# A two-pass expert layer on one core: one plain unit fewer at the start of pass one, and half of x's sums moved to VectorE

## The chip, the cores and the metric

One core of a Trainium2 chip runs the whole kernel. The metric is the time on the device in microseconds (us) of one execution; lower is better. TensorE (PE) multiplies, with its weight loads shown apart as PEld; VectorE (DVE), ScalarE (ACT) and GpSimd (POOL) do the rest; SyncE (SP) issues the transfers. Each engine works through its own instructions in the order in which they stand.

## The reference

Causal attention with decay makes x, of 2304 tokens by 512. A gate then makes P by eight rounds of normalising over experts and over tokens, and eight experts are summed:

```python
    logits = x @ w_gate
    P = np.exp(logits - logits.max())
    for _ in range(8):
        P /= P.sum(1, keepdims=True) + 1e-09
        P /= P.sum(0, keepdims=True) + 1e-09
        P *= N / E
    for e in range(E):                       # E = 8; w1 512 x 1024, w2 1024 x 512
        h = np.maximum(x @ w1[e], 0.0)
        out += P[:, e:e + 1] * (h @ w2[e])
```

## The kernel before

Every float32 product is made of three products of rounded parts (hi by hi, hi by lo, lo by hi). ScalarE makes the hi part of an operand with a copy, and VectorE or GpSimd makes the lo part by subtracting it.

The tokens are done in three passes of 768. Work goes by units: a unit is one expert e and one quarter fb of its hidden width (256 columns), so a pass has 32 units. For pass one two units (e0, fb0 and fb1) are done during the attention. Then comes the loop that this change touches: `work` holds the 30 units that are left of pass one, m = 0 for (e0, fb2), m = 1 for (e0, fb3), m = 2 for (e1, fb0) and so on.

A unit has a first product (x by w1, then relu) and a second one (h by w2, added into `acc`). In program order unit m makes its first product, then `second(*late)` makes the second product of unit m - 1. The first product comes in two kinds:

- `first_plain` (L1268) does 48 matmuls of 128x384, straight from the split w1 in `early_w["w1"]`.
- `first_fast` (L1278) does Winograd's form of Strassen's scheme: seven products of six matmuls, 42 in all. It needs sums of blocks of w1 (`weight_sums`, four instructions on GpSimd, and `split_sums`, which puts their parts into the tiles of `early_w["w1"]` and the plain blocks into `wa`), and sums of blocks of x (`token_sums`, eight instructions for each half c of the columns, and `part_sums`, which splits the four sums into the tiles `t`, here named t_4214 for c = 0 and t_4237 for c = 1). Both halves of x's sums go through one tile, `ts`.

`PLAIN` (L1374) says how many units use the plain kind. For a fast unit, `keep_w1` stores the split blocks of w1 in DRAM, and pass two and three load them from there; for the units that were not kept, `prepare_w1` makes them during pass two.

PSUM banks: a first product uses four banks in turn (`FIRST`), each free again when relu and `hl` (the lo part of h, on VectorE) have read it. The second product has six tiles of six matmuls, which use three banks in turn while e is below 2 (`GATING`): the fourth tile can begin when VectorE has added the first to `acc`, the fifth when it has added the second.

The gate is computed in between by a generator, `gate_weights`, of 51 steps. `go_on()` does one step; `first_plain` calls it four times, `second` six times, `first_fast` never. Ahead of the second product of (2, 0), at m = 7, what is left of the generator is done at once, as that product needs `prob`. Its last steps are the eighth round (`pc` on TensorE, four small instructions on VectorE that end in `prob`) and three groups of transposes of `prob` into the bank `pt` (L1182), each copied by ScalarE.

From pass two on, an own planner (`arrange`) writes the order of the instructions. Up to there the framework orders them by its own estimates, except those that are pinned.

Of the kernel before, what the change touches and what calls it, by code (L numbers as in the profile page):

```python
# [144 lines left out]
def act_sbuf(n): return 0.1 + n / 1200  # L145
# [80 lines left out]
def attention_then_moe(  # L226
# [11 lines left out]
    nc = tc.nc  # L238
# [132 lines left out]
    def step(rank, on, run, **kw):  # L371
        s = Step(rank, on, run, **kw)
        steps.append(s)
        return s
# [647 lines left out]
    with tc.manual_schedule():  # L1022
# [22 lines left out]
        a = step(-1.0, {"ACT": act_sbuf(S)}, cum_hi, after=[cum_done])  # L1045
# [42 lines left out]
    KH = KC // 2  # L1088
# [96 lines left out]
            nc.sync.dma_start(out=p_d[:, a:a + DM], in_=ps[0:E])  # L1185
            yield

    def token_sums(g, c):

        def part(k, t):  # L1190
            s = (slice(None), 2 * k + c, slice(g + t * HT, g + (t + 1) * HT))
            return x_hi[s].bitcast(F32), x_lo[s].bitcast(F32)
        (h11, l11), (h12, l12), (h21, l21), (h22, l22) = part(0, 0), part(0, 1), part(1, 0), part(1, 1)
        t = up.tile([P, 4, HT], F32, tag="ts", name="ts")
        v2, v1, v3, v4 = (t[:, n] for n in range(4))
        def pinned(**kw):
            tc.keep_in_program_order(nc.gpsimd.tensor_tensor(**kw))

        pinned(out=v3, in0=h12, in1=l12, op=ALU.add)
        pinned(out=v2, in0=h22, in1=l22, op=ALU.add)  # L1200
        yield t
        pinned(out=v1, in0=v3, in1=h11, op=ALU.subtract)
        pinned(out=v1, in0=v1, in1=l11, op=ALU.subtract)
        yield t
        pinned(out=v3, in0=v2, in1=v3, op=ALU.subtract)
        pinned(out=v2, in0=v2, in1=v1, op=ALU.subtract)
        yield t
        pinned(out=v4, in0=h21, in1=v2, op=ALU.subtract)
        pinned(out=v4, in0=v4, in1=l21, op=ALU.add)
        yield t  # L1210

    def part_sums(n, c, t):
        if t_of[n][c] is None:
            t_of[1][0] = turns_p.tile([P, 2, 4, HT], F32R, tag="turns", name="t2")
        hi, lo = (t_of[n][c][:, x] for x in range(2))
        for m in range(0, 4, 2):
            tc.keep_in_program_order(nc.scalar.copy(out=hi[:, m:m + 2], in_=t[:, m:m + 2]))
            for x in range(m, m + 2):
                tc.keep_in_program_order(
                    nc.gpsimd.tensor_tensor(out=lo[:, x], in0=t[:, x], in1=hi[:, x].bitcast(F32), op=ALU.subtract)  # L1220
                )

    def raw(nm, e, fb):
        tags = {"w1": "rw", "w2": "rq"}[nm]
        return [load_half(e, fb, nm, n, wr_p.tile([P, HALF], F32, tag=f"{tags}{n}", name="w")) for n in range(2)]

    def split_whole(nm, rs, lo_on, ws=early_w):

        hi, lo = ws[nm]
        for n, r in enumerate(rs):  # L1230
            s = slice(n * r.shape[1], (n + 1) * r.shape[1])
            nc.scalar.copy(out=hi[:, s], in_=r)  # L1232
            a = lo_on.tensor_tensor(out=lo[:, s], in0=r, in1=hi[:, s].bitcast(F32), op=ALU.subtract)  # L1233
            if lo_on is nc.gpsimd:
                tc.keep_in_program_order(a)

    def weight_sums(rs):
        t = up.tile([P, 4, KH, P], F32, tag="ws", name="ws")
        (a11, a21), (a12, a22) = ([r[:, :, n * P:(n + 1) * P] for n in range(2)] for r in rs)
        tt = nc.gpsimd.tensor_tensor  # L1240
        tc.keep_in_program_order(tt(out=t[:, 2], in0=a11, in1=a21, op=ALU.subtract))
        tc.keep_in_program_order(tt(out=t[:, 0], in0=a21, in1=a22, op=ALU.add))
        tt(out=t[:, 1], in0=t[:, 0], in1=a11, op=ALU.subtract)
        tt(out=t[:, 3], in0=a12, in1=t[:, 1], op=ALU.subtract)
        return t

    def split_sums(rs, t):
        hi, lo = wa
        k1 = rs[1].rearrange("p c (i f) -> p i c f", f=P)
        nc.scalar.copy(out=hi[:, 0], in_=rs[0][:, :, 0:P])  # L1250
        nc.scalar.copy(out=wsum[0], in_=t)  # L1251
        nc.scalar.copy(out=hi[:, 1:3], in_=k1)
        nc.gpsimd.tensor_tensor(out=lo[:, 0], in0=rs[0][:, :, 0:P], in1=hi[:, 0].bitcast(F32), op=ALU.subtract)
        for n in range(4):
            nc.gpsimd.tensor_tensor(  # L1255
                out=wsum[1][:, n], in0=t[:, n], in1=wsum[0][:, n].bitcast(F32), op=ALU.subtract
            )
        for n in range(2):
            nc.gpsimd.tensor_tensor(out=lo[:, 1 + n], in0=k1[:, n], in1=hi[:, 1 + n].bitcast(F32), op=ALU.subtract)
# [4 lines left out]
    def go_on():  # L1264
        if pending and next(pending[0], True):
            pending.pop(0)

    def first_plain(segs, hts):  # L1268
        for n, (g, w) in enumerate(segs):
            for ft in range(FB):  # L1270
                ph = bank(FIRST, [P, 512], "ph")
                hidden(ph, early_w, ft, g, w, range(KC))
                hh, hl = hts[ft][n]
                relu_hi(hh, ph, w)
                relu_lo(hl, hh, ph, w)
                go_on()
# [66 lines left out]
    def weigh(e, i):  # L1343
        to = (acc, acc_1)[e][i]
        nc.scalar.activation(out=to, in_=to, func=AF.Copy, scale=prob[:, i, e:e + 1])
# [5 lines left out]
    def second(n, e, fb, segs, hts, ws):  # L1351
        tags = GATING if e < 2 else SECOND
        tiles = [(m, g // P + tt, tt) for m, (g, w) in enumerate(segs) for tt in range(w // P)]
        for k, (m, t, tt) in enumerate(tiles):
            po = bank(tags, [P, DM], "po")
            combine(po, ws, [hts[ft][m] for ft in range(FB)], tt, range(FB))
            add_to(po, e, fb, t)
            if later_lo and k in (1, 3):
                relu_lo(*later_lo.pop(0))
            go_on()  # L1360
# [4 lines left out]
    def keep_w1(e, fb):  # L1365
        d = w1_d[e, fb] = dram.tile([len(COMBOS), P, 2, KH * P], F32, name=f"w1d{e}{fb}")
        for x in range(2):
            for ts, a, z in ((wa, 0, 3), (wsum, 3, 7)):
                nc.sync.dma_start(
                    out=d[a:z, :, x].rearrange("s p f -> p s f"),  # L1370
                    in_=ts[x].rearrange("p s k f -> p s (k f)").bitcast(F32),
                )

    PLAIN = 3  # L1374
    halves = [(0, HT), (HT, HT)]
    work = [(0, e, fb, halves) for e in range(E) for fb in range(NB)][EARLY:]
    gated = [w[:3] for w in work].index((0, 2, 0))
# [6 lines left out]
    for m, (n, e, fb, segs) in enumerate(work):  # L1384
        fast, fast_next = m >= PLAIN, m + 1 >= PLAIN
        last = m + 1 == len(work)
        if not last:
            r1 = raw("w1", *work[m + 1][1:3])
        r2 = raw("w2", e, fb)
        if m < KH:  # L1390
            sums = token_sums(0, m)
            for t in sums:
                pass
        if m == 0:
            pending.append(gate_weights())
            go_on()
        hts = hts_of[m % 2]
        if not last and fast_next:
            ws = weight_sums(r1)
        if fast:  # L1400
            first_fast(n, segs[0][0], hts, parts[m] + (t,) if m in parts and parts[m][1] else ())
        else:
            first_plain(segs, hts)
        if m < KH:
            part_sums(0, m, t)
        if not last:
            if fast_next:
                split_sums(r1, ws)
                keep_w1(*work[m + 1][1:3])
            else:  # L1410
                split_whole("w1", r1, nc.vector)
        if m in starts:
            sums = token_sums(2 * starts[m][0] * HT, starts[m][1])
            t = next(sums)
        elif any(m - k in starts for k in (1, 2, 3)):
            next(sums)
        if m in parts and not parts[m][1]:
            part_sums(*parts[m], t)
        ws = early_w
        if last:  # L1420
            ws = {"w2": [t.rearrange("p s f -> p (s f)").rearrange("p (t d) -> p t d", d=DM) for t in early_w["w1"]]}
            split_whole("w2", r2, nc.gpsimd, ws)
        if late:
            if late[:3] == (0, 2, 0):
                while pending:
                    go_on()
                for i in range(PT):
                    weigh(0, i)
            second(*late)
        if 0 <= m - 2 - gated < PT:  # L1430
            join(m - 2 - gated)
        if not last:
            split_whole("w2", r2, nc.gpsimd if fast else nc.vector)
        late = (n, e, fb, segs, hts, ws)
# [652 lines left out]
```

## Time and profile before

| | us |
|---|---|
| median of 3 runs (lowest, highest) | 1630.55 (1630.13, 1631.98) |
| time of the profiled execution | 1630.41 |
| its span in the trace | 1628.6 |
| TensorE busy in the span | 1619.9 |
| VectorE, ScalarE, GpSimd busy | 1310.4, 767.3, 1122.2 |

The profiled execution is 1.8 us longer than its span, and 0.14 us shorter than the median. An engine that is busy for less than the span matters where TensorE has to wait for it.

### The profile page before, as it was taken

What the parts mean: (1) busy time and instruction counts of PE and PEld (TensorE: products, weight loads), DVE (VectorE), ACT (ScalarE), POOL (GpSimd) and SP (SyncE); (2) the same over time, 40 slices, a digit from 0 to 9 for tenths busy, and PEclk for the clock granted to TensorE, in tenths of its full rate; (3) what the DMA queues carried; (4) which work ended last, traced back from release to release, by engine and by line L of the source; (5) the groups of instructions that cost most, each with busy time, mean ns of one, the idle gap of its engine ahead of it and who ended that gap; (6) DMA issues with size and microseconds to landing.
All of it is one profiled execution on the core that took longest, in us unless ns stands there. A gap on an engine that the chain in (4) does not pass through costs nothing.

```text
span 1628.6 us, 29751 instructions
## 1 busy us (share of the span) xinstructions
PE 1619.9 (99%) x9641; PEld 1534.1 (94%) x9641; DVE 1310.4 (80%) x2742; ACT 767.3 (47%) x1918; POOL 1122.2 (69%) x1431
## 2 busy tenths in 40 slices
PE   8999999999999999999999999999999999999999
PEld 7888889989899899899999999999999999999998
DVE  8888778776676776788898888878988888788887
ACT  8887743443333333344454444444444444344443
POOL 6556385777788887778777767666666666566675
PEclk9999999999999999999999999999999999999999
DMA  6666325655566656576777776657665555565552
GB/s 154 157 159 160 92 64 175 185 178 185 181 197 184 193 185 209 181 233 192 229 222 220 221 224 201 187 175 218 197 198 162 171 178 170 164 173 171 168 167 70
DMA packets 257025, 291.24 MB, mean 179 GB/s; under 512 B 76291, under 2 KB 168686, under 8 KB 256870
## 3 DMA queue, kind: packets, MB, share of 16 engines
q1 hardware_dynamic: 256438, 288.94, 59.5%
q8 instruction: 77, 1.26, 0.3%
q14 instruction: 78, 0.64, 0.1%
q10 hardware_dynamic: 432, 0.39, 0.1%
HBM read 222.43 MB, written 66.83 MB: 178 GB/s over the span
## 4 chain that ended last, share of the span: by engine, by line
PE 98%; ACT 0%; POOL 0%; DVE 0%; DMA 0%; issue 0%; SPq 0%
PE bankA L1838 28%; PE bankA L1736 20%; PE po L924 16%; PE ph L1292 12%; PE bankM L1736 9%; PE pv L823 3%; PE ph L904 2%; PE pt L775 2%; PE ps L614 2%; PE pq L496 1%; PE ps L660 1%; PE bankA L1889 1%; PE pt L779 0%; PE ps L607 0%; PE bankA L1922 0%; PE pg L858 0%
## 5 line engine op out<-in xcount | busy, mean ns | idle before, releaser
L1847 DVE TENSOR_TENSOR sum<-bankA,sum 128x384 f32<-128x384 f32 x406 | 224.3, 553 | 52.9 <-PE bankA L1838 51.4
L1736 PE MATMUL bankA<-t,wn 128*128 128x384 f32 x1314 | 248.3, 334 | 0.0
L924 PE MATMUL po<-early_w,hh 128*128 128x512 f32 x768 | 239.1, 392 | 0.0
L1736 PEld LDWEIGHTS bankA<-t,wn 128*128 128x128 f32 x1314 | 229.4, 188 | 0.0
L924 PEld LDWEIGHTS po<-early_w,hh 128*128 128x128 f32 x768 | 142.4, 188 | 28.7 <-issue 0.7
L1666 POOL TENSOR_TENSOR fourw<-w 128x256 f32<-128x256 f32 x124 | 91.7, 740 | 92.2 <-DMA w<-in_moe_w_dram 92.2
L924 PE MATMUL po<-early_w,hl 128*128 128x512 f32 x384 | 150.3, 391 | 0.0
L1298 DVE TENSOR_TENSOR u<-ph,u 128x384 f32<-128x384 f32 x189 | 101.9, 552 | 56.8 <-PE ph L1292 53.2
L1337 DVE SCALAR_TENSOR_TENSOR acc<-po,prob,acc 128x512 f32<-128x512 f32 x144 | 106.6, 747 | 50.5 <-PE po L924 48.8
L1838 PE MATMUL bankA<-xhi,early_w 128*128 128x384 f32 x576 | 128.3, 334 | 0.0
L1255 POOL TENSOR_TENSOR early_w<-ws,early_w 128x256 fp32r<-128x256 f32 x108 | 93.9, 898 | 39.7 <-ACT early_w L1251 38.5
L1736 PE MATMUL bankM<-xhi,wn 128*128 128x384 f32 x424 | 119.0, 334 | 0.0
L1232 ACT CAST early_w<-w 128x512 fp32r<-128x512 f32 x66 | 41.0, 622 | 161.1 <-issue 137.9
L1838 PE MATMUL bankA<-xlo,early_w 128*128 128x384 f32 x522 | 116.8, 335 | 0.0
L1529 POOL TENSOR_TENSOR w2n<-fourw,w2n 128x256 fp32r<-128x256 f32 x105 | 79.6, 761 | 43.2 <-PE bankA L1838 21.5
L1838 PE MATMUL bankA<-xhi,w2n 128*128 128x384 f32 x480 | 108.9, 334 | 0.0
L1233 POOL TENSOR_TENSOR early_w<-w,early_w 128x512 fp32r<-128x512 f32 x56 | 71.9, 1305 | 44.8 <-ACT early_w L1232 44.8
L1838 PEld LDWEIGHTS bankA<-xhi,early_w 128*128 128x128 f32 x576 | 102.4, 188 | 0.0
L1838 PE MATMUL bankA<-xlo,w2n 128*128 128x384 f32 x438 | 99.4, 334 | 0.0
L910 ACT ACTIVATE hh<-u 128x384 fp32r<-128x384 f32 x108 | 56.1, 522 | 91.4 <-DVE u L1298 91.3
L1529 POOL TENSOR_TENSOR early_w<-w,early_w 128x256 fp32r<-128x256 f32 x96 | 72.4, 760 | 37.7 <-ACT early_w L1524 37.7
L1529 POOL TENSOR_TENSOR early_w<-fourw,early_w 128x256 fp32r<-128x256 f32 x117 | 89.5, 772 | 12.0 <-ACT early_w L1524 11.3
(332 smaller groups left out, 4518.6 us busy)
## 6 DMA issues: line engine op xcount, KB each, us to landing
wn<-w1d SPq DMA_DIRECT2D x440, 256.0 KB
w<-in_moe_w_dram SPq DMA_DIRECT2D x266, 256.0 KB
w1d<-early_w SPq DMA_DIRECT2D x54, 512.0 KB
w1d<-wa SPq DMA_DIRECT2D x54, 384.0 KB
w1d<-four SPq DMA_DIRECT2D x70, 128.0 KB
dn<-cum_d SPq DMA_DIRECT2D x14, 576.0 KB
pb<-p_d SPq DMA_DIRECT2D x16, 384.0 KB
q<-in_q_dram SPq DMA_DIRECT2D x32, 128.0 KB
```

The lines of the kernel that those rows point to most:

```text
L910: nc.scalar.activation(out=hh[:, 0:w], in_=ph[:, 0:w], func=AF.Relu)
L924: nc.tensor.matmul(po[:, cols], ht[:, ts], wt[:, ft, cols], start=(ft == 0 and n == 0), stop=(ft == FB - 1 and n == 2))
L1233: a = lo_on.tensor_tensor(out=lo[:, s], in0=r, in1=hi[:, s].bitcast(F32), op=ALU.subtract)
L1255: nc.gpsimd.tensor_tensor(out=wsum[1][:, n], in0=t[:, n], in1=wsum[0][:, n].bitcast(F32), op=ALU.subtract)
L1292: nc.tensor.matmul(ps, ws[y][:, c], xs[z], start=(c == 0 and m == 0), stop=(c == KH - 1 and m == 2))
L1298: nc.vector.tensor_tensor(out=out, in0=in0, in1=in1, op=ALU.add)
L1337: a = nc.vector.scalar_tensor_tensor(out=to, in0=po, scalar=prob[:, t, e:e + 1], in1=to, op0=ALU.mult, op1=ALU.add)
L1529: eng(e).tensor_tensor(out=dst(1), in0=src(), in1=dst(0).bitcast(F32), op=ALU.subtract)
L1666: eng(en).tensor_tensor(out=vs[o](), in0=a(), in1=b(), op=op)
L1736: nc.tensor.matmul(ps, wt[:, y, c * P:(c + 1) * P], x[z], start=(start and c == 0 and m == 0), stop=(c == KH - 1 and m == 2), skip_group_c ...
L1838: nc.tensor.matmul(at_(b)[:, 0:HT], at_(w)[y][:, k * P:(k + 1) * P], at_(h)[:, z], start=(i == 0), stop=(i == 5))
L1847: nc.vector.tensor_tensor(out=to, in0=at_(b)[:, 0:HT], in1=to, op=ALU.add)
```

## The change

Two plain units in place of three, so m = 2 becomes a fast unit. Its first product needs x's sums one unit earlier. The first half's sums (c = 0) are made by VectorE at m = 0; the second half's are made by GpSimd at m = 0 too, straight behind the split of the first half, and no longer at m = 1. The w1 of unit 2 is stored by `keep_w1`, so pass two has one `prepare_w1` less.

```diff
-    def token_sums(g, c):
+    def token_sums(g, c, on=nc.gpsimd):
...
         def pinned(**kw):
-            tc.keep_in_program_order(nc.gpsimd.tensor_tensor(**kw))
+            a = on.tensor_tensor(**kw)
+            if on is nc.gpsimd:
+                tc.keep_in_program_order(a)
...
-    PLAIN = 3
+    PLAIN = 2
...
-        if m < KH:
-            sums = token_sums(0, m)
+        if m == 0:
+            sums = token_sums(0, m, nc.vector)
             for t in sums:
                 pass
...
-        if m < KH:
-            part_sums(0, m, t)
+        if m == 0:
+            part_sums(0, 0, t)
+            for t in token_sums(0, 1):
+                pass
+            part_sums(0, 1, t)
```

Line numbers of the changed kernel are 2 higher from L1197 on, so L1222 there is L1220 before.

**GpSimd, units 0 and 1.** Before, from the first half's sums to the second half's parts (ts: sums of x; t: their lo parts):

```order
L1197 TENSOR_TENSOR ts<-xhi,xlo 128x384 x2
L1197 TENSOR_TENSOR ts<-ts,xhi 128x384
L1197 TENSOR_TENSOR ts<-ts,xlo 128x384
L1197 TENSOR_TENSOR ts<-ts 128x384 x2
L1197 TENSOR_TENSOR ts<-xhi,ts 128x384
L1197 TENSOR_TENSOR ts<-ts,xlo 128x384
L1220 TENSOR_TENSOR t_4214<-ts,t_4214 128x384 x4
```

Those six rows of sums and one of parts follow once more for t_4237. Now the first half's sums are gone from here, and three lo parts of unit 2's blocks of w1 (wa) stand among the second half's sums:

```order
L1222 TENSOR_TENSOR t_4214<-ts,t_4214 128x384 x4
L1197 TENSOR_TENSOR ts<-xhi,xlo 128x384 x2
L1197 TENSOR_TENSOR ts<-ts,xhi 128x384
L1255 TENSOR_TENSOR wa_4236<-w,wa_4235 128x256
L1197 TENSOR_TENSOR ts<-ts,xlo 128x384
L1197 TENSOR_TENSOR ts<-ts 128x384
L1261 TENSOR_TENSOR wa_4236<-w,wa_4235 128x256
L1197 TENSOR_TENSOR ts<-ts 128x384
L1261 TENSOR_TENSOR wa_4236<-w,wa_4235 128x256
L1197 TENSOR_TENSOR ts<-xhi,ts 128x384
L1197 TENSOR_TENSOR ts<-ts,xlo 128x384
L1222 TENSOR_TENSOR t_4237<-ts,t_4237 128x384 x4
```

Behind these come the four sums of unit 2's w1 (ws) and then the four lo parts of them (early_w_110<-ws), as before they did for unit 3.

**ScalarE, the same units.** Before, from unit 0's last relu on (hh: relu of a first product; the CAST of t: the hi parts of x's sums, two at a time; hh100, hh110, hh101 and hh111 belong to unit 1):

```order
L910 ACTIVATE hh011_4244<-ph_4331 128x384
L1217 CAST t0_4214<-ts_4270 128x768 x2
L910 ACTIVATE hh100_4246<-ph_4398 128x384
L1156 ACTIVATE prob_78<-lg_4279,ma_4415 128x144
L910 ACTIVATE hh110_4250<-ph_4426 128x384
L910 ACTIVATE hh101_4248<-ph_4441 128x384
L1232 CAST early_w10_109<-w_4381 128x512
L1232 CAST early_w10_109<-w_4383 128x512
L910 ACTIVATE hh111_4252<-ph_4456 128x384
L1217 CAST t1_4237<-ts_4389 128x768 x2
```

And now:

```order
L910 ACTIVATE hh011_4244<-ph_4331 128x384
L1219 CAST t0_4214<-ts_4270 128x768 x2
L910 ACTIVATE hh100_4246<-ph_4409 128x384
L1252 CAST wa0_4235<-w_4396 128x256
L1156 ACTIVATE prob_78<-lg_4279,ma_4426 128x144
L1254 CAST wa0_4235<-w_4398 128x512
L910 ACTIVATE hh110_4250<-ph_4437 128x384
L1219 CAST t1_4237<-ts_4373 128x768 x2
L910 ACTIVATE hh101_4248<-ph_4452 128x384
L910 ACTIVATE hh111_4252<-ph_4467 128x384
L1253 CAST early_w10_109<-ws_4404 128x1024
```

The two CASTs of t1 now stand ahead of the last two relus of unit 1. On VectorE hl101 and hl111, which read those relus, stand right ahead of the first two adds of unit 0's second product into acc, as they did before.

**TensorE, the gate's eighth round.** Now, in the second product of (2, 0) (pc: the gate's eighth round; pt: the first transposes of prob; po: tiles of the second product):

```order
L1171 MATMUL pc_5488<-cs_5353,ones_77 128x8
L924 MATMUL po_5524<-early_w20_111,hh_4238 128x512
L924 MATMUL po_5524<-early_w21_112,hh_4238 128x512
L924 MATMUL po_5524<-early_w20_111,hl_4239 128x512
L924 MATMUL po_5524<-early_w20_111,hh_4242 128x512
L924 MATMUL po_5524<-early_w21_112,hh_4242 128x512
L924 MATMUL po_5524<-early_w20_111,hl_4243 128x512
L924 MATMUL po_5532<-early_w20_111,hh_4238 128x512
L924 MATMUL po_5532<-early_w21_112,hh_4238 128x512
L924 MATMUL po_5532<-early_w20_111,hl_4239 128x512
L924 MATMUL po_5532<-early_w20_111,hh_4242 128x512
L1182 MATMUL pt_5494<-ident_75,prob_78 8x128 x4
```

Before, the same two stood in the second product one unit ahead of that one (from pc to the first transposes):

```order
L1171 MATMUL pc_5339<-cs_5196,ones_77 128x8
L924 MATMUL po_5345<-early_w20_111,hh101_4248 128x512
L924 MATMUL po_5345<-early_w21_112,hh101_4248 128x512
L924 MATMUL po_5345<-early_w20_111,hl101_4249 128x512
L924 MATMUL po_5345<-early_w20_111,hh111_4252 128x512
L924 MATMUL po_5345<-early_w21_112,hh111_4252 128x512
L924 MATMUL po_5345<-early_w20_111,hl111_4253 128x512
L924 MATMUL po_5362<-early_w20_111,hh101_4248 128x512
L924 MATMUL po_5362<-early_w21_112,hh101_4248 128x512
L1182 MATMUL pt_5354<-ident_75,prob_78 8x128 x4
```

The eighth round has moved by one unit, to the product that itself needs prob. On VectorE the four small instructions that end in prob now stand between and behind the last two hl of the first product just ahead.

## Rows read from the trace of the kernel before

**Rows 1.** The chain that ended last, by engine, shares of the span.

```profile
PE 98%; ACT 0%; POOL 0%; DVE 0%; DMA 0%; issue 0%; SPq 0%
```

**Rows 2.** Busy time by stretch, TensorE alone: stretch, length, busy (instructions), clock, DMA.

```profile
700.00:1600.00 900.00, 899.96 (x5200) 1.00 0.64 190
```

**Rows 3.** Timeline of TensorE, units 0 to 3: start, length, instruction.

```profile
230.85 0.63 PE L924 MATMUL po<-early_w,hh 128*128 128x512 f32 x2
...
235.22 0.62 PE L924 MATMUL po<-early_w,hh 128*128 128x512 f32 x2
...
239.32 0.33 PE L904 MATMUL ph<-xhi,early_w 128*128 128x384 f32 x1
...
257.42 3.28 PE L1292 MATMUL ph<-t,early_w 128*128 128x384 f32 x18
```

**Rows 4.** Timeline of ScalarE, the same units; in brackets idle time before, and releaser.

```profile
221.59 0.48 ACT L910 ACTIVATE hh<-ph 128x384 fp32r<-128x384 f32 x1
221.97 0.82 ACT L1217 CAST t<-ts 128x768 fp32r<-128x768 f32 x1
...
234.34 0.84 ACT L1217 CAST t<-ts 128x768 fp32r<-128x768 f32 x1 [2.42 <-POOL ts L1197]
...
247.96 1.05 ACT L1251 CAST early_w<-ws 128x1024 fp32r<-128x1024 f32 x1 [1.46 <-PE ph L904]
```

**Rows 5.** Timeline of GpSimd, the same units.

```profile
213.85 2.43 POOL L1197 TENSOR_TENSOR ts<-xhi,xlo 128x384 f32<-128x384 f32 x2
...
222.89 4.37 POOL L1220 TENSOR_TENSOR t<-ts,t 128x384 fp32r<-128x384 f32 x4
227.34 2.05 POOL L1197 TENSOR_TENSOR ts<-xhi,xlo 128x384 f32<-128x384 f32 x2
...
231.41 2.90 POOL L1197 TENSOR_TENSOR ts<-ts 128x384 f32<-128x384 f32 x2
...
236.45 4.09 POOL L1220 TENSOR_TENSOR t<-ts,t 128x384 fp32r<-128x384 f32 x4
...
249.09 2.82 POOL L1255 TENSOR_TENSOR early_w<-ws,early_w 128x256 fp32r<-128x256 f32 x4 [2.46 <-ACT early_w L1251]
251.99 0.74 POOL L1241 TENSOR_TENSOR ws<-w 128x256 f32<-128x256 f32 x1
```

**Rows 6.** VectorE: its timeline, then two lines' own durations (min/median/max ns).

```profile
230.53 2.91 DVE L1233 TENSOR_TENSOR early_w<-w,early_w 128x512 fp32r<-128x512 f32 x2 [0.48 <-ACT early_w L1232]
...
249.43 0.56 DVE L913 SCALAR_TENSOR_TENSOR hl<-ph,hh 128x384 fp32r<-128x384 f32 x1 [1.97 <-ACT hh L910]
249.90 0.68 DVE L1334 TENSOR_TENSOR acc<-po,acc 128x512 f32<-128x512 f32 x1
...
L1233 DVE TENSOR_TENSOR early_w<-w,early_w x10: 676/1063/1503, 211.7 to 257.7; 128x512 fp32r<-128x512 f32 x10
...
L1571 DVE TENSOR_TENSOR four<-four,xlo x1: 906/906/906, 695.1 to 695.1; 128x384 f32<-128x384 f32 x1
```

**Rows 7.** Timelines around the gate's eighth round: TensorE, VectorE, ScalarE.

```profile
311.13 0.62 PE L924 MATMUL po<-early_w,hh 128*128 128x512 f32 x2
...
311.55 0.54 DVE L1298 TENSOR_TENSOR u<-ph,u 128x384 f32<-128x384 f32 x1
...
313.32 1.04 DVE L913 SCALAR_TENSOR_TENSOR hl<-u,hh 128x384 fp32r<-128x384 f32 x1
...
316.06 0.16 DVE L1172 TENSOR_SCALAR ca<-pc 128x8 f32<-128x8 f32 x1
...
316.69 0.31 DVE L1175 TENSOR_TENSOR prob<-prob,ca 128x144 f32<-128x144 f32 x1
...
317.03 1.34 ACT L1345 ACTIVATE acc<-acc,prob 128x512 f32<-128x512 f32 x2 [4.31 <-DVE prob L1175]
```

**Rows 8.** Weight loads of 128x128 at the kernel's start and in pass one, ns (min/median/max).

```profile
L337 PEld LDWEIGHTS warm<-ones x16: 280/333/334, 1.1 to 4.2; 128*128 128x128 f32 x16
...
L904 PEld LDWEIGHTS ph<-xhi,early_w x160: 186/188/193, 36.5 to 247.5; 128*128 128x128 f32 x160
```

## The prediction

> **What bounds the kernel now.** I read the chain that ended last first: TensorE holds 98% of it [rows 1]. A stretch of pass two then says how tightly: 899.96 of 900 us busy, with 5200 instructions at full clock [rows 2]. So whatever takes load off the other engines in pass two is worth nothing there, and only two things can move the time: matmuls that are gone, and waits of TensorE that come. The timelines of units 0 to 3 say where it could wait. TensorE runs there without a pause: unit 0's second product begins at 230.85, its fourth tile at 235.22, unit 2's first product at 239.32 [rows 3]. ScalarE and GpSimd do wait, in the order of their own instructions: ScalarE stands 2.42 us until GpSimd has made a sum of x [rows 4], VectorE stands 1.97 us until ScalarE has made a relu, and its add into acc starts only behind that [rows 6]. Both engines wait at what stands first, so I lay the changed order of each against the times of these rows. All times below are those of the trace of before, as long as nothing ahead has moved.
>
> **What is removed.** Unit 2's first product has 42 matmuls in place of 48. Eighteen of that kind in a row take 3.28 us, of which the last one's tail is about 0.33, so one follows the other after (3.28 - 0.33)/17 = 0.174 us [rows 3]. Six fewer: **-1.04 us**. That is the whole prize on TensorE. One `prepare_w1` less in pass two, on engines that TensorE does not wait for, is put at nothing: the stretch lacks only 0.04 us [rows 2]. If the cover were gone, the planner's new order there might cost or give some tenths.
>
> **The first half's sums on VectorE bring nothing.** They start when GpSimd's did, at about 214.4. VectorE's price for two inputs from SBUF at this width is not shown undisturbed: from below it is 3/4 of the 0.676 us for 512 columns, 0.51, from above the 0.906 of one such instruction beside GpSimd [rows 6]. GpSimd is idle then, so I take 0.55: eight of them and two `hl` of 0.56 in between are done near 220. At 0.906 it would be 222.8, and unit 1's first product could wait up to 2 us for its w1. But the hi copy of these sums stands on ScalarE behind the relu of unit 0's last product, which starts at 221.59, so it runs at 221.97 as before [rows 4], and GpSimd's lo parts start at 222.89 as before, end at 227.3, and the second half's sums start at 227.34 as before [rows 5]. GpSimd sits idle from 213.85 to 222.89; the VectorE work only fills a hole on another engine.
>
> **The second half's sums are needed one unit earlier, and get longer.** Before they took from 227.34 to 236.45, 9.1 us, with one pair at 2.90 instead of 2.05 [rows 5] while VectorE ran the split of w1 [rows 6]. That split is gone: 8.3. Three `wa` parts now stand among them, of the width that takes 0.74 [rows 5]: +2.2. They end at 227.34 + 10.5 = 237.8.
>
> **First new wait, at the fourth tile of unit 0's second product.** ScalarE's last two relus of unit 1 now stand behind the copies of those sums. The second copy starts at 237.8 and takes 0.84, two relus of 0.48 follow [rows 4]: 239.6 with the hand-over. VectorE's second `hl` takes 0.56, the first add into acc 0.68 [rows 6], and only this add frees the bank for the fourth tile: 240.9 in place of 235.22. **+5.7 us**. The second and third adds follow at the pace of the tiles, and tiles four to six take the 4.1 us that they took [rows 3]: the fast product begins at 245.0.
>
> **Second new wait, at its second product S2 by T2.** It needs unit 2's sums of w1, which stand on GpSimd behind the second half's parts: 237.8 + 4.1 for the parts, + 4 x 0.74 for the sums = 244.9; ScalarE's copy of 1.05 ends at 246.0 [rows 4]; two of the four lo parts, half of 2.82, end at 247.5 [rows 5]. TensorE would be there after eight matmuls, 246.4. **+1.1 us**. Both waits are one chain on GpSimd: together 6.8. From below, with GpSimd at its shortest and no hand-over, 6.0; from above, with the three `wa` parts and the sums slowed as that pair was, 8.3. Unit 3's sums then find GpSimd with time to spare, as before.
>
> **Third new wait, at the gate's eighth round.** The generator has 51 steps. Up to m = 6 it got 1 + 4 + 2 x 10 + 4 x 6 = 49 of them; now 1 + 4 + 10 + 5 x 6 = 45, which ends just short of the eighth round. So the round falls into the second product of (2, 0). Before, `prob` was ready at 317.0 behind matmuls that had nothing to do with it. Let a second product begin at E, as at 311.13: the last add of the first product ends at E + 0.96, the last `hl` at E + 3.2, with 0.6 us of another add ahead of it [rows 7]. Now that add is not there, but the four small instructions are, 0.94 us in all [rows 7]: `prob` is ready at E + 3.6. TensorE reaches the transposes after pc (0.14) and ten matmuls of 0.23 (the 8.47 us from 230.85 to 239.32, less pc, by 36 [rows 3]), at E + 2.4: +1.2. The next two groups wait for copies on ScalarE that stand behind twelve scalings of acc of 0.67 each [rows 7]: I put another 0.8 on them. **+2.0 us**, from 0.6 (VectorE undisturbed, the copies in time) to 3.0.
>
> **The sum**, against the profiled execution's own 1630.41: 1630.41 - 1.04 + 6.8 + 2.0 = **1638.2 us**; the median of the runs is 0.14 higher than that execution, which changes nothing. By its own bounds: 1636.0 to 1640.7.
>
> **The rivals.** *TensorE's clock falls in the first new wait.* TensorE has no pause near this length before, and its granted clock reads 1.00 [rows 2], so no row shows what 5.7 us of idleness does. Weight loads at the kernel's start, after an idle start, take 333 ns against 188 later [rows 8], as if the array ran slower there. If the eighteen matmuls of the last three tiles ran at half speed, they would take 4.2 us more, of which the 1.1 of the second wait is swallowed: 1641.3 at most, 1639.7 if half of them do. Against it: the column shows full clock at the start too. [...]
>
> *Only the first wait counts.* If the sums of w1 come in time, and the transposes too because VectorE is less disturbed, the time is 1630.41 - 1.04 + 5.7 = 1635.1. The estimates that the framework orders by would then be right there.
>
> *Not slower.* The second half's sums end before the fourth tile asks. The chain would have to be 5.7 us shorter, ending at 232.1: for instance if the hi copy ran as soon as VectorE's sums are there (that alone gives 3) and GpSimd did the sums in two thirds of the time. Then only the gate's round is left, 1630.41 - 1.04 + 0.6 = 1630.0 or a little more. All rows of GpSimd at this width, 1.0 us each, speak against it.
>
> *The change does not do what it says*: unit 2's blocks of w1 come late from DRAM, so that the fast unit stands anyway and nothing is gained. The loads are issued when unit 1's w1 is split, at about 222 to 223.5, and used from 230 on; if they took the 7 us in between, GpSimd would move further back and the time would be above 1640.
>
> **Chances.** Forecast 0.62; clock 0.20; only the first wait 0.12; not slower 0.04; loads late 0.02. What a measurement of this kernel can tell from no change is about 0.2%, 3.3 us. Forecast, clock, loads and nearly all of the third lie above 1633.8: slower 0.94, same 0.04, faster 0.02. The range reaches from below the third case to the upper end of the clock's: 1634.5 to 1641.5.
>
> **What would show it right or wrong.** In the changed profile TensorE should stand 5 to 6 us at the fourth tile near 235 with VectorE's add as the releaser, ScalarE should wait for GpSimd's sums at the copies of t1, and GpSimd should be idle for about 9 us from 214 on. About 1 us should be lost at the first fast product, and 1 to 3 us near the gate's last round. Pass two should take what it took. The prediction is wrong if the fourth tile starts before 237, if the first fast product waits for x's sums elsewhere, or if pass two shows idle time of TensorE.

## The result, and the profile after

| | before | after |
|---|---|---|
| median (lowest, highest), 6 runs each | 1630.48 (1629.96, 1631.98) | 1640.38 (1639.15, 1641.78) |
| profiled execution, its span | 1630.41, 1628.6 | 1640.19, 1638.4 |

The ratio is 1.0059, 95% interval 1.0049 to 1.0069: slower by 9.9 us, where 1638.2 was forecast, in a range from 1634.5 to 1641.5.

TensorE's waits of the changed kernel that before does not have (engine, tile and line, releaser: us in total, times, longest); the others stand in before's list too, or come to 0.2 us:

```profile
PE po L924 <- DVE acc L1336: 4.8, 1, 4.8
...
PE po L924 <- DVE acc L1339: 1.0, 1, 1.0
...
PE pt L1182 <- DVE prob L1175: 0.7, 1, 0.7
...
PE pt L1182 <- ACT ps L1184: 0.4, 1, 0.4
```

The first is the wait at the fourth tile of unit 0's second product, the other three lie around the gate's eighth round. A wait at S2 by T2, the second of the seven products of unit 2's fast first product, is not among them. TensorE's timeline at the first of them, which answers to [rows 3]:

```profile
231.80 0.63 PE L924 MATMUL po<-early_w,hh 128*128 128x512 f32 x2
...
235.93 0.40 PE L924 MATMUL po<-early_w,hl 128*128 128x512 f32 x1
241.16 1.22 PE L924 MATMUL po<-early_w,hh 128*128 128x512 f32 x2 [4.83 <-DVE acc L1336]
242.18 0.63 PE L924 MATMUL po<-early_w,hl 128*128 128x512 f32 x1
242.61 1.05 PE L924 MATMUL po<-early_w,hh 128*128 128x512 f32 x2
...
247.49 0.34 PE L1294 MATMUL ph<-xhi,wa 128*128 128x384 f32 x1
...
248.53 3.28 PE L1294 MATMUL ph<-t,early_w 128*128 128x384 f32 x18
```

Before the pause a matmul of 512 columns takes 0.40 us with its tail, behind it 0.63. The columns of the stretches say why. They are the stretch, its length, the busy time (and instructions) of TensorE, its weight loads, VectorE, ScalarE and GpSimd, the granted clock, and the transfers' share and GB/s:

```profile
238.00:239.00 1.00, 0.00 (x0) 0.00 (x0) 0.00 (x0) 0.77 (x2) 1.00 (x2) 0.92 0.26 88
239.00:240.00 1.00, 0.00 (x0) 0.00 (x0) 0.51 (x2) 0.83 (x3) 1.00 (x2) 0.50 0.00 0
...
246.00:247.00 1.00, 1.00 (x6) 0.81 (x5) 0.96 (x3) 0.12 (x2) 0.81 (x2) 1.00 0.59 194
231.00:256.00 25.00, 20.17 (x92) 17.52 (x91) 15.09 (x29) 8.57 (x15) 22.04 (x28) 0.86 0.32 102
700.00:1600.00 900.00, 900.00 (x5201) 899.38 (x5200) 765.68 (x1513) 409.40 (x1027) 615.85 (x782) 1.00 0.63 191
```

The granted clock fell to 0.50 while TensorE stood, and read 1.00 again from 246. The last three tiles took 6.33 us, from 241.16 to 247.49, in place of 4.1 [rows 3]. Pass two is as full as before [rows 2].

The chain that makes the fourth tile late, on ScalarE, GpSimd and VectorE, answers to [rows 4 to 6]:

```profile
222.92 1.56 ACT L1219 CAST t<-ts 128x768 fp32r<-128x768 f32 x2
...
238.23 0.83 ACT L1219 CAST t<-ts 128x768 fp32r<-128x768 f32 x1 [1.90 <-POOL ts L1197]
238.97 0.86 ACT L910 ACTIVATE hh<-ph 128x384 fp32r<-128x384 f32 x2
...
223.88 4.18 POOL L1222 TENSOR_TENSOR t<-ts,t 128x384 fp32r<-128x384 f32 x4 [9.05 <-ACT t L1219]
...
237.21 0.99 POOL L1197 TENSOR_TENSOR ts<-ts,xlo 128x384 f32<-128x384 f32 x1
...
215.30 1.01 DVE L1197 TENSOR_TENSOR ts<-xhi,xlo 128x384 f32<-128x384 f32 x2
216.24 0.55 DVE L1197 TENSOR_TENSOR ts<-ts,xhi 128x384 f32<-128x384 f32 x1
...
239.49 1.02 DVE L913 SCALAR_TENSOR_TENSOR hl<-ph,hh 128x384 fp32r<-128x384 f32 x2 [9.25 <-ACT hh L910]
240.43 1.28 DVE L1336 TENSOR_TENSOR acc<-po,acc 128x512 f32<-128x512 f32 x2
```

It reads as forecast: GpSimd idle for 9.05 us, its sums ending at 238.2, the copy, two relus, two hl, the add. All starts are 0.95 us later than in the trace of before. That comes from ahead of anything that was changed; 0.73 of it are there by TensorE's first instruction of L904, at 37.29 in place of 36.56. It begins in the first 10 us; before's row of TensorE, and after's:

```profile
4.66 0.63 PE L496 MATMUL pq<-ident,q 128*128 128x128 f32 x4
```

```profile
4.63 1.06 PE L496 MATMUL pq<-ident,q 128*128 128x128 f32 x4
```

The same four matmuls took longer, 1.06 us in place of 0.63. Of the experiments below, the sums only and the loads first show 1.06 there too, the steps spread 0.63, with the same program up to there: it goes by execution.

From start to start of TensorE's products, after against before: 0.95 at the start, 4.99 at the fourth tile, +2.23 for the three slow tiles, -1.29 for the fast product (7.28 us, against 8.57 for the plain one), +3.10 from the start of the second product of (1, 3), in which the eighth round used to be, to the end of that of (2, 1) (44.24 against 41.14), about -0.2 in all the rest: 9.78 us.

Not all of the 1.29 is saved. Before's plain product of unit 2 holds the matmul pc of the gate's second round:

```profile
241.25 0.34 PE L904 MATMUL ph<-xhi,early_w 128*128 128x384 f32 x1
241.42 0.28 PE L1171 MATMUL pc<-cs,ones 128*128 128x8 f32 x2
241.56 0.42 PE L904 MATMUL ph<-xhi,early_w 128*128 128x384 f32 x1
241.82 0.34 PE L904 MATMUL ph<-xlo,early_w 128*128 128x384 f32 x1
```

From 241.25 to 241.82 there are 0.57 us, where two steps of 0.174 would be 0.35. So pc takes 0.22 of the 8.57, and it has only moved: the stretch of +3.10 holds two rounds of the gate now (pc at 320.77 and 333.79), where it held one (315.25).

### The profile page after: what moved, and what is told of

It is laid out like the page before. It is cut to its first block, busy times and chain, and to the rows that moved or that the text cites. A ratio compares the mean times of both kernels' runs of the same rounds, so it can differ in the third digit from the quotient of the medians.

```text
span 1638.4 us, 29723 instructions
## 1 busy us (share of the span) xinstructions
PE 1623.5 (99%) x9635; PEld 1535.5 (94%) x9635; DVE 1308.6 (80%) x2750; ACT 768.2 (47%) x1913; POOL 1121.5 (68%) x1428
## 4 chain that ended last, share of the span: by engine, by line
PE 78%; DVE 0%; ACT 0%; issue 0%
PE bankA L1843 28%; PE bankA L1741 20%; PE po L924 11%; PE ph L1294 9%; PE bankM L1741 9%; PE bankA L1894 1%; PE bankA L1927 0%; PE bankM L1894 0%; DVE hl L913 0%; PE bankM L1927 0%; DVE acc L1339 0%; DVE tn L322 0%; DVE u L322 0%; ACT u L317 0%
## 5 line engine op out<-in xcount | busy, mean ns | idle before, releaser
L1300 DVE TENSOR_TENSOR u<-ph,u 128x384 f32<-128x384 f32 x196 | 105.7, 553 | 58.7 <-PE ph L1294 56.5
L1257 POOL TENSOR_TENSOR early_w<-ws,early_w 128x256 fp32r<-128x256 f32 x112 | 98.1, 906 | 34.9 <-ACT early_w L1253 30.3
L913 DVE SCALAR_TENSOR_TENSOR hl<-u,hh 128x384 fp32r<-128x384 f32 x112 | 85.0, 760 | 19.2 <-ACT hh L910 19.1
```

The costliest lines, as they stand in the source:

```text
L913: nc.vector.scalar_tensor_tensor(out=hl[:, 0:w], in0=ph[:, 0:w], scalar=0.0, in1=hh[:, 0:w].bitcast(F32), op0=ALU.max, op1=ALU.subtract)
L1257: nc.gpsimd.tensor_tensor(out=wsum[1][:, n], in0=t[:, n], in1=wsum[0][:, n].bitcast(F32), op=ALU.subtract)
L1300: nc.vector.tensor_tensor(out=out, in0=in0, in1=in1, op=ALU.add)
```

## The experiments

All start from the changed kernel, and the later ones build on each other, as told there. Times are medians; beside each stands the ratio to before, with its interval.

**Unit 1's relus ahead of the copies.** The split of the second half's sums moves behind unit 1's first product, and ScalarE's copies of unit 2's w1 stand behind its last relu.

```diff
-            part_sums(0, 1, t)
+        if m == 1:
+            part_sums(0, 1, t)
...
-                split_sums(r1, ws)
+                split_sums(r1, ws, *[tc.keep_in_program_order] * (m < PLAIN))
```

> The changed kernel, but the split of the second half's sums stands behind unit 1's first product, and ScalarE's copies of unit 2's w1 behind its last relu, so that no relu of unit 1 waits for GpSimd. Forecast's theory (GpSimd's chain sets the time, wherever it is asked for): the fourth tile of unit 0's second product follows at its pace near 236.2 with no wait, and the wait comes back at the second product of the fast unit, S2 by T2, near 241.8: GpSimd's sums of x end near 237.5, four sums of w1 at 0.76 follow, the parts of x's sums 3.9, a part of w1 0.7, and the second lo part ends near 246.6, so TensorE stands about 4.8 us there; its clock falls as it did, and the time stays at 1639 to 1641 us. Rival (only the order on ScalarE costs): once the relus stand ahead, the 5.0 us of the wait and the 2.2 us of the slower matmuls are gone: 1633.2 us.

1644.61 us (1.0086, 1.0071 to 1.0102). The fourth tile no longer waits, and the wait is back in the fast unit, though already in the first of its seven products and not at S2 by T2:

```profile
246.79 1.01 PE L1294 MATMUL ph<-xhi,wa 128*128 128x384 f32 x2 [5.71 <-POOL wa L1255]
```

GpSimd's part of w1 stands behind its parts of x's sums. The clock is at 0.50 there too, from 244 to 248. So the order on ScalarE only says where GpSimd's chain is asked for; the rival is out. That it got worse by 4 us, where 1639 to 1641 was expected, has another cause in the trace, which comes back further down: 2.5 us of waits for acc in the second product behind, while a copy of unit 3's w1 on ScalarE waited for its load with relus behind it:

```profile
254.18 0.41 ACT L1252 CAST wa<-w 128x256 fp32r<-128x256 f32 x1 [5.22 <-DMA w<-in_moe_w_dram]
```

**First half's sums back on GpSimd.**

```diff
-            sums = token_sums(0, m, nc.vector)
+            sums = token_sums(0, m)
```

> The changed kernel, but the first half's sums are made by GpSimd as before, so that nothing is left of the part on VectorE. Forecast's theory (the sums on VectorE only fill a hole on another engine, since the copy of these sums stands on ScalarE behind a relu that ends near 222): GpSimd makes them from 214.8 to about 223, its lo parts start at 223.9 or a little later, the fourth tile waits 5 us as it did, and the time is that of the change, 1640.4 us, within 0.5. Rival 1 (VectorE's sums start the chain earlier): up to 3 us more, 1643 us. Rival 2 (they slow VectorE's own work and cost something): less than 1640 us.

1640.20 us (1.0059, 1.0045 to 1.0072), against 1640.38, and the fourth tile waits as long:

```profile
240.53 1.20 PE L924 MATMUL po<-early_w,hh 128*128 128x512 f32 x2 [4.99 <-DVE acc L1336]
```

VectorE's half brings nothing and costs nothing that these times could tell.

**The sums moved, but three plain units.** `PLAIN = 3`.

> The sums of x as in the changed kernel, but three plain units as before. Forecast's theory (the wait comes from the place of the second half's copies on ScalarE, ahead of unit 1's last relus): GpSimd's sums end near 236.3, the copy at 237.2, the relus with the copies of w1 between them at 239.4, and the fourth tile starts 4.8 us late, near 241; TensorE's clock falls and costs 2.2 us; the gate's steps are those of before, so there is nothing at 318 to 362, and no product is saved: 1637.5 us. Rival (the wait comes with the fast unit 2 and its parts of w1): no wait, 1630.5 us.

1638.12 us (1.0046, 1.0032 to 1.0060); the wait is there, and the stretch from 231 to 256 reads 0.86.

```profile
241.90 1.22 PE L924 MATMUL po<-early_w,hh 128*128 128x512 f32 x2 [5.16 <-DVE acc L1336]
```

So the new place of the sums makes the wait and the clock's fall, and the fast unit is not needed for it; by the run before, it is the second half's.

**Matmuls in the pause.**

```diff
+            if (e, fb, k) == (0, 2, 3):
+                pd = psum.tile([P, DM], F32, tag=FIRST[(count[FIRST] + 1) % 4], name="pd")
+                for _ in range(18): nc.tensor.matmul(pd, hts[0][0][0][:, 0:P], ws["w2"][0][:, 0], start=True, stop=True)
             po = bank(tags, [P, DM], "po")
```

> The changed kernel with eighteen more matmuls of 128x512 ahead of the fourth tile of unit 0's second product, into a bank that is free there; nobody reads what they make. At 0.23 us each they fill 4.1 of the 5.0 us in which TensorE stood. Theory (the three tiles behind the wait took 6.3 us in place of 4.1 because the granted clock fell to half while TensorE stood): the clock stays at full, the fourth tile still starts near 241.2, the three tiles take 4.1 us, and the time is 2.2 us shorter, 1638.2 us; a wait of up to 1.1 us at S2 by T2, as forecast, may come out from under it: 1639.3 us at most. Rival (the three tiles are slow for another reason, such as the operands): 1640.4 us, with the matmuls behind the wait at 0.43 us as before.

1639.91 us (1.0058, 1.0046 to 1.0071). The stretch from 231 to 256 reads 1.00, and TensorE's timeline has:

```profile
235.34 4.26 PE L1359 MATMUL pd<-early_w,hh 128*128 128x512 f32 x18
240.39 0.73 PE L924 MATMUL po<-early_w,hh 128*128 128x512 f32 x2 [0.79 <-DVE acc L1336]
240.95 0.40 PE L924 MATMUL po<-early_w,hl 128*128 128x512 f32 x1
...
246.98 3.05 PE L1294 MATMUL ph<-t,early_w 128*128 128x384 f32 x16 [0.40 <-POOL early_w L1257]
```

The three tiles take 4.63 us in place of 6.33, so the pause did slow them. But S2 by T2 now waits for GpSimd's lo parts, as forecast: the fast product takes 7.97 us in place of 7.28, 0.5 goes in the two products behind it and another 0.5 at the gate. From the start of unit 0's first product to the end of the second product of (2, 1) the profiled executions take 149.76 us, against 149.73 of the changed kernel: nothing is left as gain, and the medians, 0.5 apart, do not tell one. The fallen clock hid the second wait; net of what stands behind it, its price in this kernel is not to be seen.

**Four more steps of the gate**, at unit 2.

```diff
+        for _ in range(4 if m == PLAIN else 0): go_on()
```

> The changed kernel with four more steps of the gate's generator at unit 2, so that by m = 6 it has done 49 steps as before. Forecast's theory (its third wait is the gate's eighth round, which came one unit later): the waits of TensorE between 318 and 362 are gone. By the forecast's term that is 2.0 us, 1638.4 us; by the changed trace, where that stretch takes 3.1 us longer than before, 1637.3 us. Rival (the stretch is slow for another reason, such as GpSimd's sums of w1 coming late there): 1640.4 us, as the change.

1638.45 us (1.0047, 1.0034 to 1.0060). The stretch of the eighth round takes 40.90 us in place of 44.24, so the whole excess was the round's place. But a matmul of another round now waits in unit 1's second product:

```profile
260.88 0.39 PE L1171 MATMUL pc<-cs,ones 128*128 128x8 f32 x2 [0.96 <-DVE cs L1166]
```

**The same steps, one in each of the units 3 to 6.** `1 if PLAIN < m < 7 else 0` in the line above.

> The changed kernel with the four more steps of the gate done one each in the units 3 to 6, in place of all four in unit 2. Theory (the four at once brought a round of the gate so close to the one before it that a matmul of it waited 1.0 us for VectorE): that wait is gone too, and the whole 3.1 us of the stretch at 318 to 362 come back: 1637.3 us. Rival (the steps cost TensorE as much wherever they stand): 1638.4 us, as with the four at once.

1636.52 us (1.0037, 1.0024 to 1.0049): that wait is gone, the stretch takes 40.80. Most of the rest of the difference to the run before is the clock, which reads 0.93 in 231 to 256 here: the three tiles take 5.67 us, in place of 6.36 there, behind the same wait of 4.83.

**A place of its own for the second half's sums** (pb and the tile of w1's sums, both free there), so that GpSimd makes them in its idle 9 us; with the copies of unit 2's w1 behind unit 1's last relu, as in the first experiment.

```diff
+            for t_1 in token_sums(0, 1, t=[pb, second_pair()]): pass
...
-            for t in token_sums(0, 1):
-                pass
-            part_sums(0, 1, t)
+            part_sums(0, 1, t_1)
```

> The changed kernel with a place of its own for the second half's sums, so that GpSimd makes them from 214.8 on, while it stood idle for 9 us, beside VectorE's of the first half; and ScalarE's copies of unit 2's w1 behind unit 1's last relu. Forecast's theory (the wait comes from the chain of sums and parts that starts only when the first half is split): the sums end at 223 to 224.5, all parts near 232.3, the sums of w1 near 237.6, so that neither the fourth tile nor S2 by T2 waits, TensorE's clock stays at full, and 5.0 + 2.2 us are gone: 1633.2 us, with the gate's 3.1 us still in it. Rival 1 (VectorE and GpSimd side by side slow each other, so that the sums end after 227): a wait of 2 to 4 us at S2 by T2, 1635 to 1638 us. Rival 2 (the w1 of unit 2 arrives late): the wait stays near 5 us at S2 by T2, 1640 us.

1637.52 us (1.0046, 1.0034 to 1.0059). Neither the fourth tile nor S2 by T2 waits, but TensorE stands at a place that no theory had named, the third matmul of unit 1's first product:

```profile
226.23 1.01 PE L904 MATMUL ph<-xhi,early_w 128*128 128x384 f32 x2 [3.26 <-DVE early_w L1235]
...
217.00 1.37 DVE L1197 TENSOR_TENSOR ts<-ts,xhi 128x384 f32<-128x384 f32 x1
...
216.62 1.33 POOL L1197 TENSOR_TENSOR pb<-ts,xhi 128x384 f32<-128x384 f32 x1
```

Side by side the two sums of these rows take 1.37 us on VectorE and 1.33 on GpSimd; those with a row of their own take 0.89 to 1.37 and 1.19 to 1.47. In the changed kernel, where each engine works alone, VectorE's take 0.55 and GpSimd's 1.0 (both in the rows above). VectorE's split of unit 1's w1 stands behind its sums, and the piece that TensorE needs ends at 226.2. The clock reads 0.50 from 224 to 228 here too, and the first products of units 0 and 1 take 24.70 us in place of 19.28. Eight sums on each engine run from 213.91 to 224.77 in this trace, 10.9 us, with two hl of VectorE among them. An estimate from the distance of their starts when alone, 0.47 and 1.0: strictly one after the other they would take 8 x (0.47 + 1.0) = 11.8, freely side by side 8 x 1.0 = 8.0.

**Both halves on VectorE**, from the kernel just above, with the split of unit 1's w1 on GpSimd and the gate's steps spread as before that.

```diff
-            for t_1 in token_sums(0, 1, t=[pb, second_pair()]): pass
+            for t_1 in token_sums(0, 1, nc.vector, [pb, second_pair()]): pass
...
+            split_whole("w1", r1, nc.gpsimd)
             part_sums(0, 0, t)
...
-            else:
+            elif m:
                 split_whole("w1", r1, nc.vector)
```

> A try at a faster one: both halves of x's sums on VectorE, the second in a place of its own, GpSimd splits unit 1's w1 in the meantime, ScalarE's copies of unit 2's w1 stand behind unit 1's last relu, and one more step of the gate in each of the units 3 to 6. Theory (the sums of both engines slowed each other, 0.55 to 1.3 us on VectorE and 1.0 to 1.3 on GpSimd, when they ran side by side; alone VectorE makes sixteen in 9 us): the sums end near 224.5, all parts near 233, nothing waits but 0 to 1 us at unit 1's first product for its w1, and the 1.3 us of the fast product are kept: 1629.2 to 1630.2 us against 1630.6 of before. Rival (GpSimd's split slows VectorE's sums as its sums did): a wait of 2 to 4 us at unit 1's first product with TensorE's clock at half behind it, 1634 to 1637 us.

1633.88 us (1.0020, 1.0011 to 1.0029). TensorE reaches the fast product without a new wait but 0.4 us at pm, the gate's transpose of its maximum, and stands within the fast product:

```profile
245.71 0.40 ACT L1252 CAST wa<-w 128x256 fp32r<-128x256 f32 x1 [4.62 <-DMA w<-in_moe_w_dram]
246.02 0.47 ACT L1304 COPY u<-ph 128x384 f32<-128x384 f32 x1
...
246.54 0.45 PE L1294 MATMUL ph<-xhi,wa 128*128 128x384 f32 x1 [1.93 <-ACT u L1304]
```

A copy of unit 3's w1 waits for its load, and the copy of the first product, whose bank TensorE needs, stands behind it.

**What stands behind that load.** Three tries on that kernel: the copy of u first (`cp` is that copy); all relus of unit 2 first, too; and with that the load ahead of the stores of unit 2's parts on SyncE's queue. Their edits, in turn (the first and the second each stand alone, the third on the second):

```diff
-                split_sums(r1, ws, *[tc.keep_in_program_order] * (m < PLAIN))
+                with tc.issue_after(cp) if m == PLAIN else ExitStack(): split_sums(r1, ws, *[tc.keep_in_program_order] * (m < PLAIN))
...
-                split_sums(r1, ws, *[tc.keep_in_program_order] * (m < PLAIN))
+                split_sums(r1, ws, *[tc.keep_in_program_order] * (m <= PLAIN))
...
         r2 = raw("w2", e, fb)
+        if m == PLAIN: keep_w1(e, fb)
...
-                keep_w1(*work[m + 1][1:3])
+                if m >= PLAIN: keep_w1(*work[m + 1][1:3])
```

> The try with both halves on VectorE, and ScalarE's copy of the fast unit's first product (u) ahead of its copies of unit 3's w1. Theory (the 1.9 us in which the fast product of unit 2 stood, and the half clock behind it, come from that copy of u, which stood on ScalarE behind a copy of w1 whose load landed at 245.7): the fast product of unit 2 takes 7.3 us in place of 11.1, the time is 3.8 us shorter, 1630.1 us, as before or up to 0.5 us less. Rival (unit 3's w1, loaded late, then stops unit 3's product S2 by T2 instead): 1632 us or more.

> The try with both halves on VectorE, with all four relus of the fast unit 2 ahead of ScalarE's copies of unit 3's w1 (the kernel with the copy of u first had only that copy ahead, and its relus stood behind the copy that waited for the load until 246.8; TensorE then waited for acc in the second product of unit 1, 2.5 us in all). Theory: those 2.5 us go too, 1632.4 - 2.5 = 1629.9 us, 0.5 to 1 us less than before. Rival (unit 3's parts of w1, now behind the relus, come late for unit 3's product S2 by T2): 1631 us or more.

> As the one before, with the load of the second half of unit 3's w1 issued ahead of the stores of unit 2's parts that stood before it on SyncE's queue and waited for GpSimd's last lo part (240.7). Theory: the load lands some 3 us earlier, GpSimd's sums for unit 3 start near 243.5 in place of 246.8, and nothing is late at unit 3: 1629.9 us if the one before had no wait left, up to 1 us less than it if it had. Rival (the load waits for its buffer, not for its place in the queue): the same as the one before.

1632.37 us (1.0012, 1.0003 to 1.0021), 1632.54 (1.0011, 1.0002 to 1.0020) and 1630.51 (0.9996, 0.9987 to 1.0005). In the first the fast product takes 7.31 us, but the second product behind it takes 11.07, in place of 8.57, with two waits for acc, as the relus still stood behind that copy. In the second the same wait comes one unit later, with unit 4's w1:

```profile
269.67 0.74 PE L924 MATMUL po<-early_w,hh 128*128 128x512 f32 x2 [1.79 <-DVE acc L1334]
```

In the third nothing of it is left; its longest waits in the attention and the units:

```profile
PE pt L775 <- ACT e L639: 0.8, 1, 0.8
PE ph L904 <- POOL early_w L1235: 0.5, 2, 0.4
PE pm L1152 <- DVE mx L1148: 0.4, 1, 0.4
```

Unit 3's sums of w1 start at 242.70 there, against 246.22 in the second, and GpSimd stood 1.21 us for that load, against 5.37: the load waited for its place in the queue, not for its buffer. All new waits but the 0.4 us of pm are out, and the time cannot be told from before's 1630.92.

**The gate's pm one step later**, on the first of the three, with one more step at unit 2 to make up for it.

```diff
-        yield
+        yield; yield
...
-        for _ in range(1 if PLAIN < m < 7 else 0): go_on()
+        for _ in range(1 if PLAIN <= m < 7 else 0): go_on()
```

> As the one before, with the gate's matmul pm one step later, since it waited 0.40 us in unit 1's first product for VectorE, which was busy with x's sums; the steps lost are made up in unit 2. Theory: 0.4 to 0.6 us less than the one before, 1629.6 us. Rival (the step only moves that wait): the same, 1630.1 us.

1632.88 us (1.0015, 1.0006 to 1.0023). The wait of pm is gone, and the first products of units 0 and 1, which pm stands in, take 19.27 us in place of 19.82: pm had cost 0.55 us. But the waits for acc behind the fast product are 2.1 us in place of 1.2, and that second product takes 12.01 in place of 11.07, so nothing of it is left in the time.

## Why the prediction was right, and where a term was off

The median lies in the range, 2.2 us above the sum. In the profiled execution, 2.0 above it, the terms stand so: the two waits with the clock +0.4, the third wait +1.1, the start +0.95, what is removed -0.25, the rest -0.2. The case that the forecast held for likeliest, two waits at full clock, did not come; the clock's case did.

- **What is removed**: -1.29 us from plain to fast product, forecast -1.04. Of the 8.57 us of the plain one 0.22 are the gate's pc, which moved into a later unit; without it 8.35 - 7.28 = 1.07 us are saved, as forecast.
- **VectorE's sums bring nothing**: shown, as far as the medians can tell, by the kernel without them, 1640.20. They took 0.55 us each, as put.
- **First new wait**: place, releaser and chain as forecast; 5.0 us, forecast 5.7, since GpSimd's sums ended 0.55 us sooner on the same axis. The kernel with only the sums moved shows that it comes from them, that with the relus ahead that it belongs to GpSimd's chain.
- **Second new wait**: forecast 1.1, not there. In its place stand 2.2 us of slow tiles, the rival that had a chance of 0.20. The forecast gave it at most 4.2, less the 1.1 of the wait that it swallows; half of the matmuls at half speed, 2.1, was close (with that, its own terms give 1639.2 and not the 1639.7 that it names). No row of before shows the half speed that this rival put; the changed profile reads a granted clock of 0.50 from 239 to 245, where the slow matmuls start 0.43 us apart, in place of 0.23. With the clock held up, 0.40 us of the wait at S2 by T2 shows. The two waits and the clock together are 7.2 us, forecast 6.8. That these are so near is luck: the clock's fall, which the sum put at nothing, made up for a first wait that was 0.7 shorter and a second one that did not show.
- **Third new wait**: mis-sized. 3.1 us, forecast 2.0 and at most 3.0. The transposes waited 0.7 us as thought (put at 1.2). What was put at 0.8 for later copies was 0.4 for the copy of ps and 1.0 for an add into acc in the unit behind, behind a relu that ScalarE did only when GpSimd had made its sums of w1; counted from pace to pace, the three are 2.6 us, and some tenths lie in the second pc of that stretch and in broken runs of matmuls. The kernel with the steps spread gives all of it back: 40.80 us, against 41.14 before.
- **Pass two**: 900.00 of 900 us busy, nothing gained or lost, as put.
- **The start**: 0.95 us of the profiled execution, in no term; of the execution, not of the change. How much of it lies in the two medians no run shows.

What stays open: in the best try, the one with the load first, the first products of units 0 and 1 take 19.84 us, in place of the 19.27 from 211.58 to 230.85 before. The kernel with pm one step later takes 19.27 there too, so those 0.57 us are pm's; the two edits were not tried together. From the start of unit 0's first product to the end of the second product of (2, 1) the best try takes 139.88 us, in place of 140.69: in one execution of each 0.8 us are gained there, but it reaches unit 0's first product 1.1 us later, at 212.66 in place of 211.58. The medians (0.4 less, in an interval that holds zero) neither show nor exclude it.

## What to carry to other kernels

A unit of work that needs its operands earlier moves a whole chain of other engines' work forward; cost the chain at its slowest engine, and then look at what stands behind each waiting instruction, since relus, hl and adds that have nothing to do with it are what TensorE meets. Giving part of the chain to an idle engine brought nothing here while the next link, a copy behind a relu, still waited (1640.38 us with it, 1640.20 without), and where both engines then ran side by side a sum took up to 1.37 us in place of 0.55 on VectorE and up to 1.47 in place of 1.0 on GpSimd, and a wait of 3.26 us came of it. When one such wait is taken out, look for the next one late: here it went from acc to the lo parts, to w1's split, to a load, to its place in a queue, and with six of them out, what was left of a prize of 1.1 us was less than the medians could tell.

## What the runs showed of the hardware

- The granted clock fell to 0.50 while TensorE stood for 4.83 us (0.92 from 238 to 239, 0.50 from 239 to 245), and in another kernel behind a pause of 1.79 us that was over already at 269.67: the stretches from 270 of the kernel with all relus first are below. Behind a pause of 1.36 us, in the kernel with pm one step later, it stayed at 1.00 (the stretches from 231 to 256 and from 256 to 272).

```profile
270.00:272.00 2.00, 2.00 (x9) 1.66 (x8) 1.52 (x4) 0.00 (x0) 2.00 (x3) 0.69 0.74 246
272.00:274.00 2.00, 2.00 (x5) 1.59 (x6) 1.21 (x5) 0.00 (x0) 0.74 (x2) 0.50 0.17 56
```

- What the fall costs is not fixed by the pause. In five kernels with a pause of 4.83 to 5.16 us at the fourth tile (the changed one, both halves on GpSimd, the sums only, four more steps at once and spread) the eighteen matmuls behind it took 5.67 to 6.36 us, against 4.10 before, where the granted clock reads 1.00: 1.6 to 2.3 us.
- In the first 10 us of the changed kernel the column reads 1.00, where four matmuls at 4.63 take 1.06 us, against 0.63 before, with the column at 1.00 too. There the column does not show what slowed them, and the rows decide.
- Sums with two inputs from SBUF, on VectorE and GpSimd at once, took 1.6 to 2.5 times as long on VectorE (0.89 to 1.37 against 0.55 us) and 1.2 to 1.5 times on GpSimd (1.19 to 1.47 against 1.0): the faster engine lost more.
